# Attention scores by fp32 matmuls on 64 array rows per head in place of stacked fp32r operands

## The chip, the cores and the metric

The kernel runs on one core of one Trainium2 chip. The metric is the device time in microseconds (us), lower is better. Three runs of the kernel before gave 1060.61, 1060.61 and 1061.64 us, median 1060.61 us.

## What is computed

Three stages follow each other. The first is attention with a compressive memory, the other two are feed-forward layers on 2304 tokens of 512 channels. All data are fp32.

```python
B, H, S, D = (4, 8, 576, 64)
scores = scale * q @ k.T                      # per head, 576 x 576, causal mask
a = exp(scores - scores.max(-1)); a /= a.sum(-1) + 1e-09
local = a @ v
q_p = phi(q)                                  # elu(q) + 1
mem_out = (q_p @ M_prev) / (q_p @ z_prev + 1e-6)
x = g * mem_out + (1 - g) * local             # g = sigmoid(beta), per head
x = (h * tanh(softplus(h))) @ w_out           # h = x @ w_in, w_in 512 x 2048
out = ((x @ w1) * (x @ w2) @ w3) @ w_out2     # 512 x 1024, 1024 x 1024, 1024 x 512
```

The change concerns the line `scores` alone.

## The kernel before, in words

**The stages.** Attention works on 16 pairs of heads (`NPAIR`), one after the other in the loop `for p in range(NPAIR + 1)`. A pair holds two heads of 64 channels; transposed, head 0 lies on partitions 0 to 63 (`UP`) and head 1 on 64 to 127 (`DN`). After the loop come the feed-forward layers (`emit_h`, `emit_x2`, `fold`, `emit_ab`, `emit_out`), which the change leaves as they are.

**One turn of the loop** overlaps three pairs. For pair p it makes the scores (`s_blocks`, `s_last`) and the normalised probabilities (`normed`); for pair p-1 it transposes the probabilities (`pt_g`) and multiplies them by v (`pv`); for pair p+1 it transposes q and k (`prep_qk`) and makes phi (`prep_phi`). In turns 2 to 11 (ten turns) `steps(background, 1)` adds one block of weight decoding (`decode`, lines 92 to 105), which is work of VectorE (DVE) and GpSimd (POOL) beside attention.

**Scores of pairs 1 to 15.** `mm` (line 59) issues every matmul. An fp32r matmul makes one pass over its columns and rounds its operands, so q and k are split into a rounded part (`hq`, `hk`) and a remainder (`lq`, `lk`). Of q·k the three terms hq·hk, lq·hk and hq·lk are kept. `prep_qk` copies each transposed k from PSUM with ScalarE (ACT, line 273), and DVE forms `lk` (line 65, `sub`). For q, ACT copies it to `qt` (line 281), POOL rounds it (`hl`, line 62) and subtracts (`hl`, line 65). Then ten DMAs of 144 KB (lines 290 to 293 and 296) build operands that fill all 128 array rows: `eqk` for head 0 and `oqk` for head 1 hold [hq; lq] against [hk; hk], and `qz` holds hq with zeros in the other head's half against `lk`. So a block of 128 query rows takes two fp32r matmuls. Blocks 0 and 1 share a PSUM bank and are 256 columns wide each; blocks 2 and 3 are 384 and 512 wide. Pair 0 skips the DMAs and takes three fp32r matmuls on 64 rows per block. The last 64 queries of both heads go together (`s_last`): `qd` holds both heads' columns with zeros elsewhere, and two halves of 288 key columns take three fp32r matmuls each.

**After the matmul**, DVE adds the mask, takes the row extreme and evicts the bank (`maxed`, the CUSTOM_DVE rows of line 361); ACT applies exp and the row sum (`expd`, line 366); `normed` adds 1e-9 to the sums (DVE, line 351), takes reciprocals (line 352) and scales the probabilities (line 356, DVE or POOL). It is called three times a turn: once per head and once for the last rows.

**Queues and buffers.** Score tiles use three PSUM banks of tag A; the transposes and `pv` use the tags X (three) and F (two). The score tiles of SBUF (`s0` to `s3`) have two buffers each, and both heads of a pair share them. All DMAs are issued by SyncE (SP), in one order. The order of instructions on each engine is chosen at build time by the tile framework's scheduler; on the chip each engine follows its own list and waits on semaphores.

## Time and profile before

| | before |
|---|---|
| median of three runs | 1060.61 us |
| profiled execution (its span) | 1060.4 us |
| TensorE matmul (PE) busy | 1014.3 us, 96% |
| TensorE weight loads (PEld) busy | 877.0 us, 83% |
| VectorE (DVE) busy | 675.2 us, 64% |
| ScalarE (ACT) busy | 541.6 us, 51% |
| GpSimd (POOL) busy | 389.9 us, 37% |
| mean DMA rate | 110 GB/s |

The time is that of the one core; the profiled execution's span is 0.2 us below the median. Shares are of the whole span, and attention is only its first 277 us; the rest is feed-forward. A matmul's record runs until its last result is written, while the next may already be streaming, so the distance from start to start tells a matmul's cost in a dense stretch, and the record's length does not. An fp32 matmul leaves two records, an fp32r matmul one.

### The profile page before, as it was taken

Reading aid. Unit: us, or ns where it says so; the run is one execution under the profiler, and the core shown is the slowest. Engines: PE = TensorE matmul, PEld = TensorE weight load, DVE = VectorE, ACT = ScalarE, POOL = GpSimd, SP = SyncE. Lnnn points to the kernel's source line nnn. Section 1 sums busy time; section 2 is a strip of 40 time slices with the busy share of each in tenths; the row PEclk is TensorE's granted clock in tenths of the full one; section 3 lists DMA queues with packets and bytes.
Section 4 is the critical chain, followed back from the end, with each engine's and each line's share of the span. In section 5 each row is a group of like instructions: output and inputs, shape, how many; then the busy total and the mean of one; then the engine's idle time right before and its main releaser. Section 6 shows DMA issues by size and latency. Waiting matters only on the chain.

```text
span 1060.4 us, 17637 instructions
## 1 busy us (share of the span) xinstructions
PE 1014.3 (96%) x6360; PEld 877.0 (83%) x6360; DVE 675.2 (64%) x1630; ACT 541.6 (51%) x1128; POOL 389.9 (37%) x393
## 2 busy tenths in 40 slices
PE   6998889889999999999999999999999999999998
PEld 5665656566798999999999999999888888888897
DVE  6599999896779889888898467767632112121111
ACT  5676667677765666666666555546232122211212
POOL 7568888784345555554655211111100000000000
PEclk9999999999999999999999999999999999999999
DMA  6777777775323343334333274444150010100101
GB/s 148 170 189 184 188 187 171 167 193 123 95 64 100 120 159 101 102 123 154 113 109 106 83 257 123 145 162 130 70 179 0 1 40 1 40 1 1 40 1 60
DMA packets 115687, 116.60 MB, mean 110 GB/s; under 512 B 71952, under 2 KB 78096, under 8 KB 115600
## 3 DMA queue, kind: packets, MB, share of 16 engines
q1 hardware_dynamic: 115600, 115.48, 38.0%
q8 instruction: 50, 0.82, 0.3%
q14 instruction: 37, 0.30, 0.1%
HBM read 71.83 MB, written 21.50 MB: 88 GB/s over the span
## 4 chain that ended last, share of the span: by engine, by line
PE 60%; DVE 20%; POOL 8%; DMA 6%; issue 4%; SPq 2%; ACT 0%; POOLq 0%; DVEq 0%
PE psA L59 24%; PE psX L59 20%; PE psF L59 12%; DVE de L104 3%; POOL da L120 2%; DMA w_dram<-da 2%; DVE da L102 2%; DVE s L361 2%; POOL da L105 2%; DVE de L103 2%; PE psF L426 2%; DVE da L98 2%; DVE da L99 2%; DVE da L100 2%; DVE s L356 1%
## 5 line engine op out<-in xcount | busy, mean ns | idle before, releaser
L59 PE MATMUL psX<-gh,wqt 128*128 128x288 f32 x1024 | 209.0, 298 | 9.4 <-DVE x L579 4.7
L105 POOL TENSOR_TENSOR da<-da,de 128x512 f32<-128x512 f32 (+1 forms) x88 | 103.0, 1174 | 292.7 <-DVE de L104 270.4
L59 PEld LDWEIGHTS psX<-gh,wqt 128*128 128x128 f32 x1024 | 165.4, 189 | 13.4 <-DVE x L579 6.2
L59 PE MATMUL psX<-gl,wqt 128*128 128x288 f32 x512 | 151.2, 296 | 0.0
L59 PE MATMUL psA<-xt,wqt 128*128 128x288 f32 x840 | 122.0, 298 | 0.0
L59 PEld LDWEIGHTS psA<-xt,wqt 128*128 128x128 f32 x840 | 116.9, 191 | 3.1 <-issue 1.0
L366 ACT ACTIVATE s<-s,acc 128x512 f32<-128x512 f32 (+4 forms) x144 | 84.3, 588 | 40.4 <-DVE acc L361 34.3
L59 PEld LDWEIGHTS psX<-gl,wqt 128*128 128x128 f32 x512 | 96.9, 189 | 0.4
L98 DVE TENSOR_SCALAR da<-draw 128x512 int32<-128x512 int32 (+1 forms) x88 | 48.4, 553 | 68.7 <-POOL wqt L65 19.1
L720 ACT COPY bs<-psA 128x512 f32<-128x512 f32 (+1 forms) x40 | 21.8, 544 | 119.0 <-PE psA L59 116.6
L59 PE MATMUL psX<-wft,room 128*128 128x512 f32 x336 | 82.1, 390 | 0.0
L59 PE MATMUL psA<-x2h,w12t 128*128 128x512 f32 (+1 forms) x288 | 79.9, 354 | 0.0
L426 PE MATMUL psF<-ident,s 128*128 128x128 f32 x400 | 69.4, 288 | 9.1 <-DVE s L356 6.0
L59 PE MATMUL psF<-xt,wqt 128*128 128x288 f32 x552 | 77.3, 295 | 0.0
L487 ACT CAST gh<-y 128x576 fp32r<-128x576 f32 x64 | 43.2, 675 | 65.3 <-DVE y L484 39.7
L721 DVE TENSOR_TENSOR bs<-bs,psA 128x512 f32<-128x512 f32 (+1 forms) x20 | 12.7, 634 | 100.1 <-PE psA L59 100.1
L59 PEld LDWEIGHTS psF<-xt,wqt 128*128 128x128 f32 x552 | 74.5, 188 | 0.1
L59 PE MATMUL psX<-pt,raw 128*64 128x64 f32 (+4 forms) x576 | 74.1, 328 | 0.0
L59 PEld LDWEIGHTS psX<-wft,room 128*128 128x128 f32 x336 | 62.6, 188 | 12.6
L361 DVE CUSTOM_DVE_ANT_0 s<-psA,mask 128x512 f32<-128x512 f32 (+3 forms) x144 | 64.1, 477 | 14.0 <-PE psA L59 10.1
L428 ACT COPY pt<-psF 128x512 f32<-128x512 f32 (+1 forms) x112 | 57.2, 541 | 26.6 <-PE psF L426 25.9
L426 PEld LDWEIGHTS psF<-ident,s 128*128 128x128 f32 x400 | 48.8, 147 | 25.4 <-issue 6.2
(130 smaller groups left out, 2214.8 us busy)
## 6 DMA issues: line engine op xcount, KB each, us to landing
draw<-in_moe_w_out_dram SPq DMA_DIRECT2D x24, 512.0 KB, 3.5
draw<-in_moe_w_in_dram SPq DMA_DIRECT2D x16, 512.0 KB, 4.3
draw<-in_moe_w_dram SPq DMA_DIRECT2D x16, 512.0 KB, 4.1
draw<-in_moe_w_dram SPq DMA_DIRECT2D x32, 256.0 KB, 3.2
w12t<-w_dram SPq DMA_DIRECT2D x8, 1024.0 KB, 8.0
out_dram<-ob SPq DMA_DIRECT2D x18, 256.0 KB, 2.0
eqk<-hl SPq DMA_DIRECT2D x30, 144.0 KB, 2.6
eqk<-hk SPq DMA_DIRECT2D x30, 144.0 KB, 2.8
```

Source lines behind the costliest of these rows:

```text
L59: nc.tensor.matmul(o, lhsT=l, rhs=r, start=start, stop=stop)
L98: V.tensor_scalar(out=ai, in0=hw, scalar1=0x7FFFFFFF, scalar2=None, op0=ALU.bitwise_and)
L99: V.tensor_scalar(out=a, in0=a, scalar1=2.0 ** -15, scalar2=122879.9921875, op0=ALU.max, op1=ALU.min)
L100: V.tensor_scalar(out=ai, in0=ai, scalar1=3, scalar2=0x3FFFFFF8, op0=ALU.logical_shift_left, op1=ALU.bitwise_and)
L104: V.scalar_tensor_tensor(out=e, in0=lw.bitcast(U32), scalar=2.0 ** -52, in1=e, op0=ALU.mult, op1=ALU.mult)
L105: nc.gpsimd.tensor_tensor(out=a, in0=a, in1=e, op=ALU.add)
L361: nc.vector.tensor_tensor_reduce(out=s, in0=o, in1=m, op0=ALU.add, op1=ALU.min, scale=-scale, scalar=init, accum_out=a,)
L366: nc.scalar.activation(out=s, in_=s, func=AF.Exp, scale=-1.0, bias=a, accum_out=r)
L426: nc.tensor.transpose(o[:, 128 * x:128 * x + 128], src[:, 128 * jb:128 * jb + 128], ident)
L428: nc.scalar.copy(out=t[:, 0:n], in_=o[:, 0:n])
L487: nc.scalar.copy(out=gh, in_=y[i])
L720: nc.scalar.copy(out=bs, in_=pb)
```

## The change

Transposed q and k are kept in fp32 (`qt`, `kt`), copied from PSUM by ACT as before. Each score block of a head is one fp32 matmul on that head's 64 array rows; the two heads' matmuls are written alternately, into two banks. The rounding, the subtractions, the tiles `hl`, `hk`, `lk`, `eqk`, `oqk`, `qz` and the ten DMAs per pair are gone; pair 0 goes the same way as the others. `qd` is half as wide, and each half of `s_last` is one fp32 matmul on 128 rows. Block 0 is 128 columns wide in place of 256. The score tiles in SBUF have four buffers in place of two. `normed` is called once for all eight blocks, after the scores of both heads.

```diff
@@ -218,10 +218,6 @@
             hv = slice(64 * e, 64 * e + 64)
             nc.vector.tensor_copy(out=ogp[hv, :, 8], in_=gv[hv, :, e])
 
-    qz = ep.tile([128, 2, S], F32R, name="qz")
-    for e, hv in enumerate((DN, UP)):
-        nc.gpsimd.memset(f(qz[hv, e]), 0.0)
-
     s4 = ap_.tile([128, 640], F32, name="s4")
     nc.gpsimd.memset(s4[:, S:640], 0.0)
 
@@ -263,49 +259,16 @@
             evac(slice(c0, c1), pt[:, 0:c1 - c0])
 
     def prep_qk(p):
-        hl = ep.tile([128, 2, S], F32R, tag="hl", name="hl", bufs=1)
-        hq, lq = hl[:, 0], hl[:, 1]
-        hk = ep.tile([128, S], F32R, tag="hk", name="hk", bufs=2)
-        lk = ep.tile([128, S], F32R, tag="lk", name="lk", bufs=2)
-
-        def split(h, l):
-            def go(cs, o):
-                nc.scalar.copy(out=h[:, cs], in_=o)
-                sub(l[:, cs], o, h[:, cs])
-            return go
-
-        if p == 0:
-            trans(st[p]["q"], split(hq, lq))
-        else:
-            t = ep.tile([128, S], F32, tag="qt", name="qt", bufs=2)
-            trans(st[p]["q"], lambda cs, o: nc.scalar.copy(out=t[:, cs], in_=o))
-            pool_round(hq, t)
-            sub(lq, t, hq, nc.gpsimd)
-        trans(st[p]["k"], split(hk, lk))
-        if p > 0:
-
-            E = ep.tile([128, 2, S], F32R, tag="eo", name="eqk", bufs=2)
-            O = ep.tile([128, 2, S], F32R, tag="eo", name="oqk", bufs=2)
-            for t, a, z in ((E, UP, DN), (O, DN, UP)):
-                dm(out=f(t[a, 0]), in_=f(hq[a]))
-                dm(out=f(t[z, 0]), in_=f(lq[a]))
-                dm(out=f(t[a, 1]), in_=f(hk[a]))
-                dm(out=f(t[z, 1]), in_=f(hk[a]))
-
-            for e, hv in enumerate((UP, DN)):
-                dm(out=f(qz[hv, e]), in_=f(hq[hv]))
-            st[p]["Q"] = (E[:, 0], O[:, 0])
-            st[p]["K"] = (E[:, 1], O[:, 1])
-        st[p]["L"] = lk
-        st[p]["h"] = hl
-
-        t4 = ep.tile([128, 2, 2, 64], F32R, tag="qd", name="qd", bufs=1)
+        for nm in "qk":
+            t = ep.tile([128, S], F32, tag=nm + "t", name=nm + "t", bufs=2)
+            trans(st[p][nm], lambda cs, o: nc.scalar.copy(out=t[:, cs], in_=o))
+            st[p][nm + "t"] = t
+
+        t4 = ep.tile([128, 2, 64], F32, tag="qd", name="qd", bufs=2)
         nc.gpsimd.tensor_tensor(
-            out=t4, in0=f(hl[:, :, None, 512:S]).to_broadcast([128, 2, 2, 64]),
-            in1=own[:, None].to_broadcast([128, 2, 2, 64]), op=ALU.mult,
+            out=t4, in0=st[p]["qt"][:, None, 512:S].to_broadcast([128, 2, 64]), in1=own, op=ALU.mult
         )
-        st[p]["Q4"] = t4
-        st[p]["H"] = hk
+        st[p]["q4"] = t4
         st[p]["s"] = {}
         st[p]["sum"] = ap_.tile([128, 9], F32, tag="sum", name="sum", bufs=2)
         st[p]["acc"] = ap_.tile([128, 10], F32, tag="acc", name="acc", bufs=2)
@@ -346,7 +309,7 @@
 
         d = st[p]
         og = ogp[:, p % NP]
-        sl = slice(xs[0][1], 8, 2) if len(xs) > 1 else slice(8, 9)
+        sl = slice(0, 8) if len(xs) > 1 else slice(8, 9)
         rv = d["sum"][:, sl]
         nc.vector.tensor_scalar(out=rv, in0=rv, scalar1=1e-9, scalar2=None, op0=ALU.add)
         nc.vector.reciprocal(out=rv, in_=rv)
@@ -365,31 +328,21 @@
     def expd(s, a, r):
         nc.scalar.activation(out=s, in_=s, func=AF.Exp, scale=-1.0, bias=a, accum_out=r)
 
-    def s_blocks(p, e, blocks):
+    def s_blocks(p, blocks):
         d = st[p]
-        KL = d["L"]
-        if p > 0:
-            Q, K1 = d["Q"][e], d["K"][e]
-        r = slice(64 * e, 64 * e + 64)
-        pt = psA()
-        for j, ib in enumerate(blocks):
-            W = max(128 * ib + 128, 256)
-            o = pt[:, 256 * j:256 * j + W]
-            i_ = slice(128 * ib, 128 * ib + 128)
-            if p == 0:
-                mm(o, d["h"][r, 0, i_], d["H"][r, 0:W], True, False)
-                mm(o, d["h"][r, 1, i_], d["H"][r, 0:W], False, False)
-                mm(o, d["h"][r, 0, i_], KL[r, 0:W], False, True)
-            else:
-                mm(o, Q[:, i_], K1[:, 0:W], True, False)
-                mm(o, qz[:, e, i_], KL[:, 0:W], False, True)
+        pt = [psA() for _ in range(2)]
         for j, ib in enumerate(blocks):
             W = 128 * ib + 128
-            s = ap_.tile([128, W], F32, tag=f"s{ib}", name=f"s{ib}", bufs=2)
-            x = 2 * ib + e
-            maxed(s, pt[:, 256 * j:256 * j + W], mask[:, 384 - 128 * ib:512], 3e38, d["acc"][:, x:x + 1])
-            expd(s, d["acc"][:, x:x + 1], d["sum"][:, x:x + 1])
-            d["s"][ib, e] = s
+            for e, r in enumerate((UP, DN)):
+                mm(pt[e][:, 256 * j:256 * j + W], d["qt"][r, 128 * ib:128 * ib + 128], d["kt"][r, 0:W], True, True)
+        for j, ib in enumerate(blocks):
+            W = 128 * ib + 128
+            for e in range(2):
+                s = ap_.tile([128, W], F32, tag=f"s{ib}", name=f"s{ib}", bufs=4)
+                x = 2 * ib + e
+                maxed(s, pt[e][:, 256 * j:256 * j + W], mask[:, 384 - 128 * ib:512], 3e38, d["acc"][:, x:x + 1])
+                expd(s, d["acc"][:, x:x + 1], d["sum"][:, x:x + 1])
+                d["s"][ib, e] = s
 
     def s_last(p):
         d = st[p]
@@ -398,9 +351,7 @@
         for z in range(2):
             o = psA()[:, 0:CH]
             cs = slice(CH * z, CH * z + CH)
-            mm(o, d["Q4"][:, 0].rearrange("p e c -> p (e c)"), d["H"][:, cs], True, False)
-            mm(o, d["Q4"][:, 1].rearrange("p e c -> p (e c)"), d["H"][:, cs], False, False)
-            mm(o, d["Q4"][:, 0].rearrange("p e c -> p (e c)"), d["L"][:, cs], False, True)
+            mm(o, d["q4"].rearrange("p e c -> p (e c)"), d["kt"][:, cs], True, True)
             maxed(s[:, cs], o, mask4 if z else mask[:, 0:CH], acc[:, 9:10] if z else 3e38, acc[:, 9 - z:10 - z])
         expd(s, acc[:, 8:9], d["sum"][:, 8:9])
         d["s"][4] = s4
@@ -508,21 +459,17 @@
             ek.close()
             wps[0] = wk.enter_context(tc.tile_pool(name="wp", bufs=1, side="right"))
         if now:
-            s_blocks(p, 0, (3,))
+            s_blocks(p, (3,))
         if old:
             for i in (4, 2, 3):
                 pt_g(p - 1, i)
         if new:
             prep_qk(p + 1)
         if now:
-            s_blocks(p, 0, (2,))
+            s_blocks(p, (2,))
             if p == 0:
                 prep_phi(0)
-            s_blocks(p, 0, (0, 1))
-            normed(p, [(i, 0) for i in range(4)])
-            s_blocks(p, 1, (0, 1))
-            s_blocks(p, 1, (3,))
-            s_blocks(p, 1, (2,))
+            s_blocks(p, (0, 1))
         if p + 2 < NPAIR:
             load_pair(p + 2)
         if old:
@@ -532,11 +479,11 @@
                 emit_h((0, 0, 0))
             pt_g(p - 1, 6)
         if now:
+            normed(p, [(i, e) for e in range(2) for i in range(4)])
             pt_g(p, 1)
         if 2 <= p < 12:
             steps(background, 1)
         if now:
-            normed(p, [(i, 1) for i in range(4)])
             s_last(p)
         if old:
             pv(p - 1)
```

The first place is TensorE in a turn of the steady stretch, before the change: the scores of head 1 (`oqk`, `lk`/`qz`), the last rows (`qd`), and the next pair's head 0 (`eqk`); `psF<-ident,s` are transposes of probabilities, `psX<-pt,raw` are `pv`.

```order
L59 MATMUL psA<-lk,qz 128x256
L59 MATMUL psA<-oqk 128x256
L59 MATMUL psA<-lk,qz 128x256
L59 MATMUL psX<-pt,raw 64x64 x7
L59 MATMUL psA<-oqk 128x512
L59 MATMUL psA<-lk,qz 128x512
L59 MATMUL psX<-pt,raw 64x64
L262 MATMUL psX<-ident,raw 128x128 x2
L59 MATMUL psA<-oqk 128x384
L59 MATMUL psA<-lk,qz 128x384
L59 MATMUL psX<-pt,raw 64x64 x2
L59 MATMUL psA<-hk,qd 128x288 x2
```

And TensorE in a turn of the changed kernel, with buffer numbers: `psA_1152` and `psA_1153` are the 512-wide blocks of the two heads of one pair, `psA_1207` and `psA_1208` the 384-wide ones.

```order
L59 MATMUL psA_1152<-kt_988,qt_978 128x512
L377 MATMUL psF_1053<-ident_66,s4_114 128x128
L59 MATMUL psX_1093<-pt_971,raw_433 64x384
...
L258 MATMUL psX_1144<-ident_66,phie_1126 128x128 x3
L59 MATMUL psA_1153<-kt_988,qt_978 128x512
L59 MATMUL psA_1207<-kt_988,qt_978 128x384
L59 MATMUL psA_1208<-kt_988,qt_978 128x384
L258 MATMUL psX_1184<-ident_66,raw_1030 128x128 x2
```

The number of score matmuls per pair (without the last rows) falls from 16 to 8. The two heads of a block do not always stand side by side: the 512-wide blocks here have 27 other matmuls between them, since the second waits for a bank, while head 1's 512 columns and head 0's 384 do follow each other. Over the whole attention the 128 score matmuls of 64 rows stand in 59 runs.

The second place is SP's queue in turn 2 to 3, before:

```order
L296 DMA qz<-hl 64x576 x2
L244 DMA raw<-in_q_dram 128x4x64 x2
L246 DMA raw<-in_q_dram 128x2x64
L244 DMA raw<-in_k_dram 128x4x64 x2
L290 DMA eqk<-hl 64x576
L291 DMA eqk<-hl 64x576
```

And the same queue now:

```order
L92 DMA draw<-in_moe_w_in_dram 128x1024
L240 DMA raw<-in_v_dram 128x4x64 x2
L246 DMA raw<-in_v_dram 64x2x64 x2
L240 DMA raw<-in_q_dram 128x4x64 x2
L242 DMA raw<-in_q_dram 128x2x64
L249 DMA zr<-in_z_prev_dram 128x128
```

The loads of q, k, v, z and of the weights (`draw`) no longer stand behind copies that wait for POOL and TensorE.

## Rows read from the trace of the kernel before

**Rows 1.** Busy time by stretch: us, busy of each engine, PEclk, DMA share, GB/s.

```profile
0.00:50.00 50.00, 40.05 (x211) 29.91 (x211) 30.98 (x98) 31.06 (x82) 33.73 (x50) 0.97 0.69 161
50.00:225.00 175.00, 154.00 (x1006) 104.05 (x1005) 162.78 (x451) 117.22 (x338) 138.26 (x143) 0.97 0.76 183
225.00:277.00 52.00, 50.06 (x352) 35.91 (x351) 38.72 (x135) 38.95 (x115) 26.14 (x30) 1.00 0.49 117
277.00:1060.00 783.00, 770.17 (x4797) 707.16 (x4795) 442.74 (x950) 354.32 (x594) 191.79 (x172) 1.00 0.27 90
```

**Rows 2.** Timeline of DVE, the eviction that ends the scores of pairs 2, 11, 15.

```profile
61.42 0.51 DVE L361 CUSTOM_DVE_ANT_0 s<-psA,mask,acc 128x288 f32<-128x288 f32 x1
...
219.38 0.51 DVE L361 CUSTOM_DVE_ANT_0 s<-psA,mask,acc 128x288 f32<-128x288 f32 x1
...
277.00 0.51 DVE L361 CUSTOM_DVE_ANT_0 s<-psA,mask,acc 128x288 f32<-128x288 f32 x1
```

**Rows 3.** Groups by line on DVE, 20 to 275 us: busy, mean ns, idle before.

```profile
L65 DVE TENSOR_TENSOR lk<-psX,hk 128x256 fp32r<-128x256 f32 (+1 forms) x30 | 12.9, 441 | 4.8 <-ACT hk L273 4.7
```

**Rows 4.** Groups by line and shape on DVE, 50 to 225 us.

```profile
L351 DVE TENSOR_SCALAR sum<-sum 128x4 f32<-128x4 f32 x20 | 10.7, 537 | 1.2 <-ACT s L366 1.2
...
L352 DVE RECIPROCAL sum<-sum 128x4 f32<-128x4 f32 x20 | 3.4, 170 | 0.2
```

**Rows 5.** Line 351 alone: duration min/median/max in ns.

```profile
L351 DVE TENSOR_SCALAR sum<-sum x48: 118/160/1390, 17.6 to 279.1; 128x4 f32<-128x4 f32 x32, 128x1 f32<-128x1 f32 x16
```

**Rows 6.** Groups by line on POOL, 20 to 275 us.

```profile
L65 POOL TENSOR_TENSOR hl<-qt,hl 128x576 fp32r<-128x576 f32 x15 | 22.0, 1464 | 0.7
...
L303 POOL TENSOR_TENSOR qd<-hl,own 128x256 fp32r<-128x256 f32 x15 | 13.1, 874 | 1.9 <-PE psF L426 1.3 <-DMA oqk<-hl 0.5
...
L62 POOL TENSOR_SCALAR hl<-qt 128x576 fp32r<-128x576 f32 x15 | 10.7, 716 | 7.0 <-ACT qt L281 4.4 <-DMA oqk<-hl 1.2 <-issue 1.2
```

**Rows 7.** Timeline of PE, a dense run of scores: start, length, record.

```profile
271.98 0.28 PE L59 MATMUL psA<-lk,qz 128*128 128x256 f32 x1
272.10 0.40 PE L59 MATMUL psA<-oqk 128*128 128x512 f32 x1
272.33 0.40 PE L59 MATMUL psA<-lk,qz 128*128 128x512 f32 x1
272.56 0.34 PE L59 MATMUL psA<-oqk 128*128 128x384 f32 x1
272.74 0.34 PE L59 MATMUL psA<-lk,qz 128*128 128x384 f32 x1
...
275.26 0.29 PE L59 MATMUL psA<-lk,qd 128*128 128x288 f32 x1
275.39 0.43 PE L59 MATMUL psA<-hk,qd 128*128 128x288 f32 x2
```

**Rows 8.** Timeline of PE, fp32 matmuls of `pv` and transposes.

```profile
152.10 1.13 PE L59 MATMUL psX<-phi,mr 128*128 128x512 f32 x2
153.15 1.07 PE L59 MATMUL psX<-pt,raw 128*64 128x512 f32 x2
...
154.86 1.07 PE L59 MATMUL psX<-pt,raw 128*64 128x512 f32 x4
...
157.37 0.28 PE L426 MATMUL psF<-ident,s 128*128 128x128 f32 x1
157.58 0.54 PE L59 MATMUL psX<-pt,raw 128*64 128x384 f32 x2
```

**Rows 9.** DMA issues: count, KB each, median us to landing.

```profile
eqk<-hl SPq DMA_DIRECT2D x30, 144.0 KB, 2.6
```

**Rows 10.** Waits of SP's queue, whole span: us in total, times, longest.

```profile
SPq L290 <- PE psA L59: 22.7, 20, 3.8
```

**Rows 11.** Waits of all engines, 20 to 275 us.

```profile
PE psA L59 <- DMA eqk<-hk: 2.4, 3, 1.0
```

**Rows 12.** The chain that ended last, its longest DMA piece in attention.

```profile
141.59 5.88 DMA eqk<-hk
```

## The prediction

> **What bounds the kernel now.** I read the busy times by stretch first. They split the span in four [rows 1]: a start of 50 us, a steady stretch of attention from 50 to 225 us, the end of attention to 277 us, and the feed-forward layers. In the last, TensorE is busy 770.17 of 783 us; the change touches nothing there, so I take it as a block of fixed length, and attention's gain or loss passes on in full. Inside attention the bound changes. From 50 to 225 us DVE is busiest, 162.78 of 175 us (93%), TensorE has 154.00 (88%), POOL 138.26. From 225 to 277 us TensorE has 50.06 of 52 us and DVE 38.72: no weight decoding is left in those turns.
>
> The timeline gives a turn's length [rows 2]. The last eviction of pair 2's scores stands at 61.42 us, that of pair 11 at 219.38: nine turns of 17.55 us, with decoding. From there to pair 15 at 277.00 are four turns of 14.4 us, without. So of a turn of 17.55 us DVE is busy 0.93 x 17.55 = 16.3. TensorE's busy share overstates it, since a record is about 0.28 us long where the next one starts 0.12 us later [rows 7]; what a turn costs TensorE when little holds it up is 50.06/52 x 14.4 = 13.9 us. DVE with 16.3 is the bound of ten turns, TensorE with 13.9 that of the last four, and about 1.2 us of each decoding turn is stall.
>
> **What leaves DVE.** Per pair the two subtractions for `lk` go: 30 took 12.9 us [rows 3], so 0.86 us. One of the two `normed` calls for the blocks goes, with a 128x4 addition and a reciprocal: 537 and 170 ns in the steady stretch [rows 4], so 0.71 us. The addition alone shows how much of this is waiting: its median is 160 ns and its longest 1390 ns [rows 5], and it reads and writes SBUF only, beside a POOL that is busy 79% of the stretch [rows 1]. POOL loses the rounding, the subtraction and half of `qd`: 22.0 + 10.7 + 13.1/2 = 39 us over 15 pairs [rows 6], 2.6 us of the 13.9 us that it is busy per turn. How much DVE gains from a quieter POOL no row tells. It may be nothing, and at most all 2.6 us. I take 0.5: the addition lost 537 - 160 = 377 ns twice per turn, other DVE operations on SBUF must lose too, and a fifth of POOL's work goes. DVE then has 16.3 - 0.86 - 0.71 - 0.5 = 14.2 us per decoding turn.
>
> **What TensorE does in place of it.** Before: from start to start an fp32r matmul of 512 columns takes 0.23 us, of 384 0.18, of 256 0.12, of 288 0.13 [rows 7]. A head is 2 x 0.23 + 2 x 0.18 + 4 x 0.12 = 1.30 us, the last rows 6 x 0.13 = 0.78, a pair 3.4 us. For sixteen pairs that is 54 us (pair 0, with three terms, costs more, but stands in the start, where TensorE has time).
>
> After: an fp32 matmul of 512 columns leaves two records, which keep TensorE from 152.10 to 153.15 and from 153.15 to beyond 154.16, so 1.0 us [rows 8]. A part of this is a change of tile shape: transposes on 128x128 follow each other every 0.11 us, but from the one at 157.37 to the first 128x64 matmul at 157.58 there are 0.21 us [rows 8], so a change of shape costs 0.10. Without it 512 columns take 0.87 us or 1.7 ns per column. Counted in the order, the 128 score matmuls have 40,960 columns: one after the other 70 us. The last rows add 32 x 288 columns, 15.7 us. Changes of shape between neighbours rise from 158 to 262 in attention, 104 x 0.10 = 10.4 us. Sum: 96 us.
>
> Against this stands that two heads use different halves of the array's rows. Whether such matmuls run at the same time no row shows. The nearest is `pv`, where the heads use different halves of the columns: two matmuls, 512 and 384 wide, end 1.07 us after the first starts, as long as one of 512 alone needs (two and four records, both 1.07 us) [rows 8]. So I take full overlap inside a run. In the order, where runs are broken by waits for banks, overlap leaves about 30,000 of the 40,960 columns: 51 us. Then TensorE has 51 + 15.7 + 10.4 = 77 us in place of 54, 23 us more, 1.4 us per pair; without overlap 96 - 54 = 42 us, 2.6 per pair. The Trainium skill, "TensorEngine Tiling (Array Packing)", section "Theoretical Speedup", gives up to 2x for a contraction of 64 or less; by that the 70 us would be 35, and the sum below would come out some 7 us faster. The order speaks against this: only heads that stand next to each other can share the array.
>
> **What leaves the queues.** 150 DMAs of 144 KB go [rows 9], each half a microsecond of SP's time. SP's queue stood 22.7 us in 20 waits on TensorE before `eqk` could be overwritten [rows 10], and the loads of raw q and k and of weights stood behind. TensorE itself waited for these copies only 2.4 us in three places [rows 11], yet one of them is 5.88 us of the chain that ended last [rows 12]. The chain shows no sum that I may subtract: where a copy is gone, an eviction or exp is late next. I count this as part of the stall, with the two further score buffers, which let a pair's evictions start before the transposes of the previous pair have read theirs. ACT has the same copies as before, so nothing there.
>
> **The sum.** In the ten decoding turns DVE falls to 14.2 us, and TensorE rises to 13.9 + 1.4 = 15.3 us and becomes the longer one. With the old stall of 1.2 us a turn takes 16.5. But now two engines are nearly equally full, and scores, evictions, exp and transposes hand work to and fro between them; a stall of 1.5 is as likely, for the copies' latency is gone at the same time. I take 16.8: 0.75 us less per turn, -7.5 us. The last four turns were TensorE's: 4 x 1.4 = +5.6 us, of which about 1 us returns from the copies. The start (pairs 0 and 1) has 10 us in which TensorE stands still [rows 1], some of it while the first copies are built; I take -3 us there, with the price of 2 x 1.4 us inside what is idle. Together -7.5 + 4.6 - 3 = -6 us against the profiled span of 1060.4. It lies 0.2 us below the median of the runs, so 1060.6 - 6 = **1054.6 us**. Between a stall of 0.7 and one of 2 us per turn the forecast's own range is 1047 to 1059.
>
> **The rivals.** A difference of 0.2% is 2.1 us, about what a measurement of this kernel can tell from no change.
>
> *TensorE takes the place of DVE* (slower). The place is the score runs; the price is that the two heads don't overlap, or that the second mostly waits for its bank until the first is done. Then a turn has 13.9 + 2.6 = 16.5 us of TensorE; with 1.2 us of stall it is 17.7, as now, the last four turns cost 4 x 2.6 = 10 us and the start 2: 1073 us. With overlap and a stall of 2.5 us per decoding turn the ten turns gain nothing, and 1063 comes out. It decides from the point where TensorE's addition exceeds some 2 us per decoding turn. For it: the fp32 passes are plain in the rows, and TensorE is at 96% in the last turns. Against it: the `pv` rows.
>
> *The full gain.* The queues and POOL were the real cause of the stall, and the array overlaps more than the order suggests, or hides its changes of shape. Then a decoding turn falls to about 15.5 us, -20 us, the last turns stay as they are, and the start gives 3: 1037 us. For it: the 5.88 us of one copy on the chain, and DVE additions of up to 1390 ns. Against it: 104 more changes of shape. A doubling as the page on tiling has it would lie between this case and mine.
>
> *Nothing to measure.* Gains in ten turns and losses in the others cancel, or POOL and DVE give their time to ACT's exp: 1060.6 within 2 us.
>
> **How the numbers follow.** My forecast 45%, the full gain 13%, nothing 12%, slower 30%. Of the forecast's range almost all lies more than 2.1 us below the median. So faster 0.57, same 0.12, slower 0.31. For eight in ten the range must reach into both other cases: down to 1038, where the full gain ends, and up to 1074, past the case without overlap.
>
> **What the changed profile would show.** Right: attention ends 5 to 10 us sooner; from 50 to 225 us DVE falls below 88% busy and TensorE rises above it; line 351's mean shrinks; the two heads' matmuls start within a few tens of ns of each other where they are neighbours, and both end together; a DMA share of about 0.4 in place of 0.76. Wrong: the second head's records start only when the first head's end; turns of 17 us and more with TensorE near 96%; or turns below 15.5 us; or a feed-forward part whose length changes by more than 2 us.

## The result, and the profile after

The changed kernel takes 1049.32 us (median of four runs, 1048.44 to 1049.86) against 1061.05 us of the kernel before on the same chip (1060.61 to 1061.64). The ratio is 0.9893, with an interval from 0.9879 to 0.9907: 11.7 us less. The sign and the range of the prediction hold; the gain is about twice the 6 us that it named. The profiled execution has a span of 1048.1 us, before 1060.4; the last window below ends behind the changed program's end.

Busy time by stretch of the changed kernel, columns as in [rows 1]:

```profile
0.00:50.00 50.00, 42.67 (x194) 24.68 (x194) 36.18 (x102) 30.06 (x84) 34.48 (x49) 1.00 0.57 135
50.00:225.00 175.00, 175.00 (x1097) 104.39 (x1096) 151.40 (x441) 129.78 (x378) 110.39 (x127) 1.00 0.39 96
225.00:277.00 52.00, 51.62 (x339) 33.14 (x338) 29.55 (x97) 34.23 (x93) 14.19 (x19) 1.00 0.13 38
277.00:1060.00 783.00, 754.83 (x4693) 694.94 (x4693) 436.17 (x926) 344.70 (x577) 186.38 (x168) 1.00 0.27 88
```

From 50 to 225 us TensorE goes from 154.00 of 175 us busy to all 175.00, DVE from 162.78 to 151.40 (87%), POOL from 138.26 to 110.39, and the DMA share from 0.76 to 0.39. The granted clock goes from 0.97 to 1.00. The chain of waits inside attention says the same without the weakness of busy shares. First the kernel before, then the change, both cut to 20 to 265 us, shares by line (PE is TensorE; `psA` are scores, `psX` with L59 `pv` and the memory's matmuls, `psF` and the other `psX` transposes):

```profile
by line: PE psA L59 11.6%; PE psX L59 9.7%; DVE s L361 8.4%; DVE s L356 6.4%; PE psF L426 5.9%; issue 5.4%; PE psX L262 4.0%; DMA draw<-in_moe_w_in_dram 3.4%; DVE phie L323 2.9%; DVE da L102 2.7%; DVE dn L329 2.4%; DVE sum L351 2.4%; DMA eq
```

```profile
by line: PE psX L59 34.6%; PE psA L59 32.7%; PE psF L377 20.7%; PE psX L258 12.1%; issue 0.0%
```

Before, no engine carries the chain: TensorE's four groups here are 31%, and DVE, DMAs and issue alternate with them. After, the four groups of TensorE are the whole of it. One engine, never waiting, now sets the length of attention.

The evictions that end the scores of pairs 2, 11 and 15, in DVE's timeline of the change [rows 2]:

```profile
58.71 0.51 DVE L324 CUSTOM_DVE_ANT_0 s<-psA,mask,acc 128x288 f32<-128x288 f32 x1
...
200.84 0.52 DVE L324 CUSTOM_DVE_ANT_0 s<-psA,mask,acc 128x288 f32<-128x288 f32 x1
...
263.80 0.52 DVE L324 CUSTOM_DVE_ANT_0 s<-psA,mask,acc 128x288 f32<-128x288 f32 x1 [2.66 <-PE psF L377]
```

Pair 2 ends 2.7 us sooner. The nine decoding turns up to pair 11 take (200.84 - 58.71)/9 = 15.79 us each in place of 17.55, together 15.8 us less. The last four take 62.96/4 = 15.74 us in place of 14.4, together 5.3 us more. Turns with and without decoding are equally long now: decoding is hidden. Attention ends 13.2 us sooner, more than the 5 to 10 us that the prediction named as its sign; what follows takes 784.3 in place of 783.4 us.

TensorE's timeline of the change shows the overlap (start, length, operation, and how many records stand in the row; one head's fp32 matmul leaves two):

```profile
150.71 1.12 PE L59 MATMUL psA<-kt,qt 64*128 64x512 f32 x2
...
154.52 0.33 PE L59 MATMUL psX<-pt,raw 128*64 128x64 f32 x2
154.78 0.33 PE L377 MATMUL psF<-ident,s 128*128 128x128 f32 x1
155.03 0.33 PE L59 MATMUL psX<-pt,raw 128*64 128x64 f32 x2
...
167.30 1.13 PE L59 MATMUL psA<-kt,qt 64*128 64x512 f32 x4
```

Two records of one head take 1.12 us, four records of both heads 1.13 us: two heads on opposite halves of the rows cost as much as one. The three rows between show the price of changing shape: matmuls of 64 columns and transposes alternate every 0.26 us, while transposes in a row follow each other every 0.11 us [rows 8]. So a change costs some 0.15 us here, not the 0.10 us of the prediction.

That holds for the whole timeline. Divide TensorE's records between the evictions of pairs 2 and 15 into runs of one tile shape. A run lasts longer than its columns take in a dense stretch, by a median of 0.16 us for 128x128 tiles, 0.15 for 128x64 and 0.20 for 64x128 (runs without overlap), or about 0.16 per change. The prediction had only the wait before the next matmul's start; the first matmul after a change is longer as well.

### The profile page after: what moved, and what is told of

Its sections match the earlier page's. It is cut to its first block, busy times and chain, and to the rows that moved or that the text cites. A ratio compares the mean times of both kernels' runs of the same rounds, so it can differ in the third digit from the quotient of the medians.

```text
span 1048.1 us, 17122 instructions
## 1 busy us (share of the span) xinstructions
PE 1024.1 (98%) x6320; PEld 857.2 (82%) x6320; DVE 653.3 (62%) x1564; ACT 538.8 (51%) x1128; POOL 345.4 (33%) x361
## 4 chain that ended last, share of the span: by engine, by line
PE 75%; DVE 12%; POOL 6%; issue 3%; DMA 2%; ACT 1%; SPq 1%; DVEq 0%; POOLq 0%
PE psA L59 29%; PE psX L59 25%; PE psF L59 12%; PE psF L377 5%; PE psX L258 3%; POOL da L120 2%; DVE de L104 2%; POOL da L105 2%; DVE da L99 1%; DVE da L100 1%; DVE de L103 1%; DVE gl L65 1%; DVE da L98 1%; DVE da L102 1%; DMA w_dram<-da 1%
## 5 line engine op out<-in xcount | busy, mean ns | idle before, releaser
L59 PE MATMUL psX<-gh,wqt 128*128 128x288 f32 x1024 | 208.4, 297 | 11.9 <-DVE x L524 6.2
L59 PEld LDWEIGHTS psX<-gh,wqt 128*128 128x128 f32 x1024 | 164.7, 188 | 16.1 <-DVE x L524 7.4
L59 PE MATMUL psX<-gl,wqt 128*128 128x288 f32 x512 | 150.7, 295 | 0.0
L59 PE MATMUL psA<-xt,wqt 128*128 128x288 f32 x840 | 121.8, 297 | 0.6 <-DVE y L435 0.6
L59 PEld LDWEIGHTS psA<-xt,wqt 128*128 128x128 f32 x840 | 116.3, 190 | 3.7 <-DVE y L435 1.5
L329 ACT ACTIVATE s<-s,acc 128x384 f32<-128x384 f32 (+3 forms) x144 | 84.8, 593 | 36.4 <-DVE acc L324 22.1
L59 PEld LDWEIGHTS psX<-gl,wqt 128*128 128x128 f32 x512 | 96.5, 188 | 0.4
L59 PE MATMUL psX<-wft,room 128*128 128x512 f32 x336 | 82.1, 390 | 0.0
L59 PE MATMUL psA<-x2h,w12t 128*128 128x512 f32 (+1 forms) x288 | 79.9, 354 | 0.0
L324 DVE CUSTOM_DVE_ANT_0 s<-psA,mask 128x512 f32<-128x512 f32 (+2 forms) x144 | 65.0, 478 | 21.3 <-PE psA L59 19.1
L59 PE MATMUL psF<-xt,wqt 128*128 128x288 f32 x552 | 77.3, 295 | 0.0
L59 PE MATMUL psX<-pt,raw 128*64 128x64 f32 (+4 forms) x576 | 75.0, 328 | 0.0
L59 PE MATMUL psA<-kt,qt 64*128 64x384 f32 (+3 forms) x256 | 71.6, 490 | 3.0 <-DVE acc L324 2.5
L59 PEld LDWEIGHTS psF<-xt,wqt 128*128 128x128 f32 x552 | 74.5, 188 | 0.1
L59 PEld LDWEIGHTS psX<-wft,room 128*128 128x128 f32 x336 | 62.6, 188 | 12.6
L59 PE MATMUL psA<-x2s,w12t 128*128 128x512 f32 x288 | 67.9, 389 | 0.0
```

The lines of the kernel that those rows point to most:

```text
L59: nc.tensor.matmul(o, lhsT=l, rhs=r, start=start, stop=stop)
L324: nc.vector.tensor_tensor_reduce(out=s, in0=o, in1=m, op0=ALU.add, op1=ALU.min, scale=-scale, scalar=init, accum_out=a,)
L329: nc.scalar.activation(out=s, in_=s, func=AF.Exp, scale=-1.0, bias=a, accum_out=r)
```

## The experiments

The theory after the result was that TensorE alone sets a turn, so that its own list decides: score columns left after overlap, at 1.7 ns each, and changes of tile shape between neighbours, at 0.10 us each (both prices from the prediction, and so in the expectations). The rivals were that one of the other parts carries the gain: the score buffers, the copies, POOL's work, DVE's work. Each variant's list was counted over attention. "Pair 2" is when its scores end, the turns are worked out as above, and "half clock" is the work that TensorE lost there to its lower clock, the sum over the turns between the evictions of pairs 0 and 15 of their length times (1 - granted clock). The last column is the counted list against the changed kernel's, with a change at 0.10 us and, behind the stroke, at the measured 0.16. The kernel before, measured beside each variant, took between 1058.96 and 1061.46 us, and the ratio is to that; so differences of two variants' medians, unless they were measured side by side, are good to some 2.5 us.

| kernel | median us | ratio to before [interval] | pair 2 | decoding turn | last turns | changes / columns | half clock | counted, 0.10 / 0.16 |
|---|---|---|---|---|---|---|---|---|
| before | 1061.05 | | 61.42 | 17.55 | 14.41 | 158 / | 6.8 | |
| changed | 1049.32 | 0.9893 [0.9879, 0.9907] | 58.71 | 15.79 | 15.74 | 262 / 30,336 | 0 | 0 |
| two buffers | 1069.96 | 1.0095 [1.0068, 1.0121] | 60.16 | 17.29 | 16.82 | 285 / 34,304 | 0 | +9 / +10 |
| old order, 2 buffers | 1065.19 | 1.0062 [1.0042, 1.0082] | 56.98 | 17.44 | 17.12 | 271 / 40,704 | 0 | +18.5 / +19 |
| old order, 4 buffers | 1051.20 | 0.9925 [0.9896, 0.9954] | 58.37 | 15.82 | 16.24 | 219 / 37,376 | 0 | +7.6 / +5 |
| 128 rows | 1050.63 | 0.9907 [0.9887, 0.9927] | 57.96 | 16.23 | 15.66 | 144 / 40,960 | 0 | +6 / -1 |
| copies back | 1057.07 | 0.9962 [0.9948, 0.9975] | 62.55 | 16.40 | 15.45 | 242 / 32,000 | 0 | +1 / 0 |
| POOL back | 1058.57 | 0.9992 [0.9970, 1.0015] | 64.68 | 16.91 | 15.53 | 247 / 30,720 | 6.8 | -1 / -2 |
| DVE back | 1051.55 | 0.9919 [0.9884, 0.9954] | 59.58 | 15.99 | 15.95 | 269 / 29,056 | 3.4 | -1.5 / -1 |
| decoding to 15 | 1048.82 | 0.9900 [0.9874, 0.9926] | 58.40 | 15.96 | 15.55 | 261 / 30,976 | 0 | +1 / +1 |
| before, less room | 1072.83 | 1.0117 [1.0084, 1.0149] | 62.85 | 18.29 | 14.93 | 140 / | 13.7 | |
| the same, 4 buffers | 1072.37 | 1.0106 [1.0073, 1.0138] | 65.64 | 17.92 | 15.63 | 150 / | 10.2 | |
| before, 3 buffers | 1074.95 | 1.0144 [1.0116, 1.0172] | 60.90 | 18.85 | 15.23 | 140 / | 13.7 | |
| two `s4` | 1046.69 | 0.9869 [0.9853, 0.9886] | 53.25 | 16.08 | 15.39 | 217 / 27,008 | 1.7 | -10 / -13 |

### Two score buffers again

```diff
-                s = ap_.tile([128, W], F32, tag=f"s{ib}", name=f"s{ib}", bufs=4)
+                s = ap_.tile([128, W], F32, tag=f"s{ib}", name=f"s{ib}", bufs=2)
```

> The changed kernel with two buffers for each score tile again, nothing else. Theory (TensorE bounds every turn of the changed kernel): what counts is the order that the buffers allow. It has 285 changes of tile shape in place of 262 and some 34,300 columns with overlap in place of 30,300, so TensorE gets 2.3 + 6.8 = 9 us more work and the time is about 1058 us. Rival (the gain came from DMAs and DVE, the buffers did nothing): 1049 us, within 2.

It takes 1069.96 us: 20.6 us more than the change, slower than the kernel before, and 12 us above the expected 1058. The waits of all engines, first the changed kernel from 20 to 265 us, then this one from 20 to 275 (total, times, longest):

```profile
DVE s L324 <- PE psA L59: 18.2, 19, 2.1
...
DVE s L324 <- PE psF L377: 4.6, 3, 2.7
```

```profile
DVE s L324 <- PE psF L377: 39.1, 20, 2.7
...
DVE s L324 <- PE psA L59: 25.2, 15, 2.3
```

The eviction waits 39.1 us in place of 4.6 for `psF`, that is for the transposes (line 377) that read the old contents of its score tile. The counted list explains 9 or 10 of the 20.6 us. TensorE's timeline says where the rest is: from pair 2's to pair 15's eviction this kernel takes 17.8 us more than the changed one. The runs of score matmuls last 60.6 us in place of 48.2, so 12.4 us are overlap lost and changes of shape; 3.4 us are TensorE standing still. TensorE's four groups are 82% of this kernel's chain in attention, so evictions that come late have a part in it.

### The operands alone, in the order of before

Scores are made head by head and `normed` is called once per head, as before, but by fp32 matmuls on 64 rows; then the same with four buffers.

```diff
-    def s_blocks(p, blocks):
+    def s_blocks(p, e, blocks):
...
-            s_blocks(p, (0, 1))
+            s_blocks(p, 0, (0, 1))
+            normed(p, [(i, 0) for i in range(4)])
+            s_blocks(p, 1, (0, 1))
+            s_blocks(p, 1, (3,))
+            s_blocks(p, 1, (2,))
```

> The fp32 operands alone: the changed kernel's qt and kt, no copies, but the scores written head by head, two buffers per score tile and normed per head, as before. In this order no two heads' matmuls overlap (40,700 of 40,960 columns one after the other). Theory (the operands free DVE, POOL and the queues, but only with four buffers per score tile can TensorE be kept busy; the x1 run lost 20 us with two): no better than the kernel before, 1058 to 1070 us. Rival (removing copies, POOL's and DVE's work is the whole gain, whatever the buffers): 1052 us or less.

> As y1_old_order, with four buffers per score tile: fp32 operands, head by head. 219 changes of tile shape in place of 262, and 37,400 columns in place of 30,300 after overlap. Theory (buffers decide, overlap and changes of shape about cancel, as in x4_128rows): 1049 to 1054 us. Rival (the overlap of the two heads carries the gain): TensorE has 12 - 4 = 8 us more, 1057 us and up.

With two buffers 1065.19 us: without the buffers and without the alternation, the new operands lose 0.6%, although the copies and the work of POOL and DVE are gone. With four buffers, measured beside it, it takes 1051.20 us, 14.0 less; both as expected. The chain of the first, 20 to 265 us, is TensorE alone, as in the changed kernel:

```profile
by line: PE psA L59 37.4%; PE psX L59 31.4%; PE psF L376 19.8%; PE psX L258 11.5%
```

So here the buffers don't act by ending a wait on the chip. With more buffers the build time's scheduler writes another order for TensorE: 52 fewer changes of shape and 3,328 fewer columns outside an overlap, counted 5.2 + 5.7 = 10.9 of the 14.0 us, and 8.3 + 5.7 = 14.0 at the measured 0.16 us per change.

### The scores without overlap

`qt` holds each head's q with zeros in the other half, written by two ACT copies of 64 partitions. Each head is one fp32 matmul on all 128 rows.

```diff
-                mm(pt[e][:, 256 * j:256 * j + W], d["qt"][r, 128 * ib:128 * ib + 128], d["kt"][r, 0:W], True, True)
+                mm(pt[e][:, 256 * j:256 * j + W], d["qt"][:, e, 128 * ib:128 * ib + 128], d["kt"][:, 0:W], True, True)
```

> The changed kernel with q kept with zeros in the other head's half, so that each score matmul is fp32 on all 128 rows: no overlap of heads, but no change of tile shape for scores either. Theory (overlap is worth 70 - 51 = 19 us of TensorE, the 118 changes of shape that go are worth 12): 7 us slower, about 1056 us, with TensorE without idle time. Rival 1 (TensorE is not the bound): 1049 within 2. Rival 2 (changes of shape cost more than their 0.10 us, by draining the queue): faster than 1049.

It takes 1050.63 us, 1.3 more than the change, with intervals that overlap; I had expected 7 more. All 40,960 columns are paid for (18 us more), but the score matmuls now have the shape of the transposes and 118 changes go: 11.8 us less at 0.10 us each, which leaves 6 us that are not there, but 18.9 at the measured 0.16. So the second rival was right that a change costs more than 0.10 us, though the kernel is not faster. The first rival's time came out too, but not its reason: TensorE is busy 144.91 of the 146.0 us of the decoding turns. Here 512 columns take 0.86 us from start to start, 152.16 to 153.02, without a change on either side; in the changed kernel it was 1.06, 150.71 to 151.77, with one on each:

```profile
152.16 1.02 PE L59 MATMUL psA<-kt,qq 128*128 128x512 f32 x2
153.02 0.27 PE L390 MATMUL psF<-ident,s 128*128 128x128 f32 x1
```

The overlap is real, but what it saves here is paid back in shape changes.

### The copies back

Ten DMAs of 144 KB per pair into tiles that nobody reads.

```diff
+            for g in range(2):
+                w = ep.tile([128, 2, S], F32, tag="cp", name="cp", bufs=2)
+                for nm, j in (("qt", 0), ("kt", 1)):
+                    dm(out=w[UP, j], in_=st[p][nm][UP])
+                    dm(out=w[DN, j], in_=st[p][nm][DN])
+            for hv in (UP, DN):
+                dm(out=cq[hv], in_=st[p]["qt"][hv])
```

> The changed kernel with ten copies of 144 KB per pair from qt and kt into tiles that nothing reads: the old load on SP's queue and on the DMA engines, without anyone who waits for the copies. Theory (the copies cost only through those who waited for them): within 2 us of 1049. Rival (the load itself and the loads queued behind it made the stall of 1.2 us per turn): turns of 17 us again, 10 us or more slower, 1059 us and up.

It takes 1057.07 us, 7.8 more, between the two expectations, with a counted list hardly longer. Nobody reads the copies, so their cost comes through the queue and its order: SP waits 11.5 us in nine places for ACT's copy of k before it may issue a copy, and the loads stand behind. Line 98, the first DVE operation of decoding, by shape from 50 to 225 us (busy, mean ns, idle before), in the changed kernel and here:

```profile
L98 DVE TENSOR_SCALAR da<-draw 128x512 int32<-128x512 int32 x8 | 4.0, 502 | 0.1
```

```profile
L98 DVE TENSOR_SCALAR da<-draw 128x512 int32<-128x512 int32 x10 | 5.2, 517 | 9.9 <-DMA draw<-in_moe_w_in_dram 6.3 <-DMA draw<-in_moe_w_dram 2.5 <-DMA draw<-in_moe_w_out_dram 0.7
```

DVE now stands 9.9 us for raw weights that queue behind the copies. The three longest pieces of the chain, 20 to 265 us, are a copy and two such loads:

```profile
51.21 8.03 DMA cp<-qt
...
143.34 4.80 DMA draw<-in_moe_w_out_dram
...
178.84 6.05 DMA draw<-in_moe_w_dram
```

### POOL's work back

POOL rounds q and subtracts, as before, into a tile that nobody reads.

```diff
+        if p > 0:
+            w = ep.tile([128, 2, S], F32R, tag="pw", name="pw", bufs=1)
+            pool_round(w[:, 0], st[p]["qt"])
+            sub(w[:, 1], st[p]["qt"], w[:, 0], nc.gpsimd)
```

> The changed kernel with POOL's rounding and subtraction of q back (2.1 us per pair), results unread. Theory (TensorE is the bound, DVE has about 2 us of slack per turn): at most 3 us slower, 1049 to 1052. Rival (a busy POOL stretches DVE's work on SBUF and DVE is still close to the bound): DVE's 128x8 addition and the scalings get longer, turns grow by 0.5 to 1 us, 1057 to 1063 us.

It takes 1058.57 us, 9.3 more, as the rival had it, with a list counted 1 or 2 us shorter. The profiled execution is 7 us above this median: its clock was 0.50 from 45 to 59 us, which the other turns don't show, so only turns after pair 2 are compared. They give 9 x 1.12 - 4 x 0.21 = 9.2 us, about the whole difference. The nine decoding turns, first of the changed kernel, then here, columns as above:

```profile
58.70:200.80 142.10, 142.10 (x899) 85.44 (x899) 127.61 (x366) 105.73 (x306) 95.70 (x110) 1.00 0.41 102
```

```profile
64.70:216.90 152.20, 145.61 (x913) 86.89 (x909) 141.01 (x368) 105.22 (x306) 113.49 (x123) 1.00 0.38 96
```

TensorE stands still for 6.6 us, and DVE is busy 13.4 us more with as many operations of its own program, at 93% of the time, the share that it had in the kernel before. Two DVE operations of decoding, by shape from 50 to 225 us, in the changed kernel and here:

```profile
L102 DVE SCALAR_TENSOR_TENSOR da<-draw,da 128x512 int32<-128x512 int32 x9 | 10.2, 1128 | 0.1
...
L104 DVE SCALAR_TENSOR_TENSOR de<-draw,de 128x512 f32<-128x512 uint32 x9 | 6.0, 664 | 0.0
```

```profile
L102 DVE SCALAR_TENSOR_TENSOR da<-draw,da 128x512 int32<-128x512 int32 x9 | 12.4, 1373 | 0.1
...
L104 DVE SCALAR_TENSOR_TENSOR de<-draw,de 128x512 f32<-128x512 uint32 x9 | 9.2, 1023 | 0.0
```

Both take longer, by 245 and 359 ns, though DVE's own program has not changed. Not all do: the 128x8 addition, which the rival named, takes 247 ns in place of 266, and the scaling of 384 columns 689 in place of 811. Over all, DVE's operations are slower beside a busier POOL; but DVE's order was chosen anew too, and the runs don't separate the price of this from work queued behind POOL's two steps.

### DVE's subtractions back

```diff
+                if nm == "k":
+                    nc.vector.tensor_tensor(out=w[:, cs], in0=o, in1=t[:, cs], op=ALU.subtract)
```

> The changed kernel with DVE's two subtractions of k per pair back, results unread (0.86 us of DVE per pair). Theory (DVE and TensorE are now nearly equally full, so every DVE microsecond counts in part, as POOL's 2.1 us counted 9 us in x3_pool): 4 to 9 us slower, 1053 to 1058 us. Rival (TensorE alone bounds the turns): 1049 within 2.

It takes 1051.55 us, 2.2 more; the ratio's interval overlaps the changed kernel's, so the effect is small or nothing. I had expected 4 to 9: DVE has 15.79 - 14.2 = 1.6 us of room per turn now, and 0.86 us fit into it.

### Decoding spread to the last turns

```diff
-        if 2 <= p < 12:
+        if 2 <= p < 16:
```

> The changed kernel with one block of weight decoding in turns 12 to 15 too. Theory (in those turns TensorE is the bound and DVE has over 6 us free per turn, so the decoding costs nothing there; the feed-forward part then has four blocks less to decode while TensorE waits some 16 us in it): 2 to 6 us faster, 1043 to 1047 us. Rival (the decoding costs as much in attention as in the earlier turns, and the feed-forward part gains nothing): 1049 to 1054 us.

It takes 1048.82 us, 0.5 less, which is no difference. Turns with and without decoding were already equal, so attention stays as long (264.22 against 263.80), and what follows shortens by 2.3 us in this profile, 782.0 against 784.3. The 2 to 6 us that I had expected did not come.

### Four buffers with the stacked operands

With the stacked operands kept, four buffers don't fit: the pool of attention's early tiles then wants 55.3 KB per partition where 46.3 are left. To have room I took a buffer each from `qt`, `phie`, raw q/k and raw v of the kernel before (less room), and added the score buffers to that. A third kernel takes `qt` and `phie` alone and has three score buffers.

```diff
-                a = ap_.tile([128, NB, 2, D], F32, tag="vr", name="raw", bufs=3)
+                a = ap_.tile([128, NB, 2, D], F32, tag="vr", name="raw", bufs=2)
...
-            t = ep.tile([128, S], F32, tag="qt", name="qt", bufs=2)
+            t = ep.tile([128, S], F32, tag="qt", name="qt", bufs=1)
```

> The kernel before with 9.75 KB per partition freed: one buffer in place of two for qt and for phi's exp, three in place of four for raw q and k, two in place of three for raw v. Only the control for z1_room_4. Both theories: 1059 to 1065 us, no faster than before.

> z0_room with four buffers per score tile: stacked fp32r operands and copies as before, the buffers of the changed kernel. Theory (the kernel before is bound by DVE, 93% busy, which waits for a score buffer only 2.9 us in all; the buffers help only where TensorE is the bound, as between y1 and y3): within 3 us of z0_room. Rival (the buffers are the whole gain, whatever the operands, and the stacked ones even cost TensorE less): 10 us or more faster than z0_room, 1051 us or less.

> The kernel before with three buffers per score tile, room made by one buffer in place of two for qt and for phi's exp alone. Theory: within 3 us of the kernel before. Rival: 5 us or more faster than before.

Room alone costs 11 us against the kernel before beside it (1061.46), where I had expected at most 4, so the comparison stands on a disturbed base. On it, four buffers give nothing: 1072.37 against 1072.83 us, as the theory had it. The kernel with three takes 1074.95, 13.5 more than the kernel before, and not within 3. The stretch from 50 to 225 us, first with less room alone, then with four buffers, columns as above:

```profile
50.00:225.00 175.00, 154.22 (x993) 105.34 (x994) 153.63 (x437) 115.22 (x330) 127.10 (x134) 0.94 0.73 173
```

```profile
50.00:225.00 175.00, 152.63 (x998) 102.93 (x998) 151.81 (x435) 113.73 (x326) 128.40 (x135) 0.96 0.70 170
```

TensorE and DVE stay at 87 to 88% busy and the clock falls below 1.00. Here something other than score buffers holds the turns: fewer buffers for raw data, the copies and POOL's work are all there, and which of them it is is not shown. Whether the kernel before would gain from four buffers with nothing taken from it stays open, since there is no room for it.

### A second buffer for the last rows

`s4`, the score tile of the last 64 queries, was the one left with a single buffer.

```diff
-    s4 = ap_.tile([128, 640], F32, name="s4")
+    s4_ = [ap_.tile([128, 640], F32, name=f"s4{i}") for i in range(2)]
...
-        s = s4[:, 0:S]
+        s = s4_[p % 2][:, 0:S]
```

> The changed kernel with two buffers in place of one for the probabilities of the last 64 queries (s4). Theory (TensorE is the bound in all turns of the changed kernel, and a further score buffer acts through the order that it allows): 217 changes of tile shape in place of 262 and 27,000 columns in place of 30,300, so TensorE has 4.5 + 5.6 = 10 us less; DVE, at 87%, then takes a part of it back, 1039 to 1045 us. Rival (TensorE is not what bounds the turns, or the order's counts say little of the time): 1049 within 2.

It takes 1046.69 us, 0.9869 of before, the best of all; but the interval overlaps that of the change, and I had expected 1039 to 1045. Pair 2 ends 5.5 us sooner. Attention ends at 259.55 us in place of 263.80, and what follows takes 786.8 us in place of 784.3. Two of the nine decoding turns take 17.5 and 19.6 us; the busy times of about these two stretches:

```profile
84.00:102.00 18.00, 16.28 (x96) 10.23 (x95) 17.24 (x42) 11.07 (x35) 12.02 (x15) 0.91 0.44 107
102.00:122.00 20.00, 18.82 (x114) 10.58 (x115) 18.21 (x49) 13.14 (x38) 12.80 (x15) 1.00 0.39 95
```

In the first DVE is busy 17.24 us and TensorE 16.28, with 3.4 us at half clock. Shorten TensorE's list by a counted 10 us, and TensorE waits again in some turns, with DVE the busier engine in one of them; that DVE binds them is likely, but not shown.

## Why the prediction came out as it did

**The bound.** Right: TensorE takes over all turns. Its last four turns went from 14.4 to 15.74 us, +1.34 where the sum of 51 + 15.7 + 10.4 us had said +1.4 per pair. This agreement is in part luck. The last four turns, before and after:

```profile
219.40:277.00 57.60, 54.50 (x372) 38.30 (x371) 44.32 (x151) 42.73 (x127) 30.36 (x36) 1.00 0.52 122
```

```profile
200.80:263.80 63.00, 63.00 (x404) 38.54 (x404) 35.76 (x131) 44.26 (x130) 20.74 (x27) 1.00 0.12 27
```

TensorE's busy time rose by 2.1 us per turn, and 0.8 us of idle time went. The assumed overlap, for which there were only the `pv` rows, holds for neighbours. The start with pair 2 gave 2.7 us; the forecast was 3 and, for pair 2's turn, 0.75. The feed-forward part changed by 0.9 us, within the 2 allowed.

**The terms that were mis-sized** are the stall of the decoding turns and the change of shape, in opposite directions. TensorE was put at 15.3 us and a stall of 1.5 on top, for 16.8; measured are 15.79. The stall is gone: TensorE is busy in all 142.10 us of these nine turns. TensorE's own turn is longer than 15.3, for a change of shape costs 0.16 us and not 0.10: the 104 more of them are 16.6 us in place of 10.4, the sum per pair is 1.8 in place of 1.4, and 13.9 + 1.8 = 15.7. The prediction's own rows held a sign of it: the 512 columns from 152.10 to 153.15 take 1.05 us with a change behind them [rows 8], 0.18 more than the 0.87 without. Nine turns gave 15.8 us in place of 6.8, and this error of 9 us is more than the 6 us by which the profiled span differs from the forecast; the start, the last turns and the feed-forward part gave some back, 1.0, 0.7 and 0.9 us.

**The step behind it.** The prediction said that now "two engines are nearly equally full" and hand work to and fro, and so kept a stall of 1.5 us; but DVE, busy 90% of these turns, never made TensorE wait. The kernel with two buffers has such long turns, 17.29 us with decoding, but not for that reason alone: its last turns, where DVE is busy 56% of the time, take 16.82. The step that failed is the one that counted the two further score buffers only "as part of the stall", with no price. They are worth 14 us with the old order and 20.6 with the new one, more than the whole gain, and in both cases much of it is the order of TensorE's list and not a wait that ends. They come with the operands: the removed tiles leave the SBUF that they need. Without them the new operands are slower than the old ones.

**DVE** fell to 87% as forecast (below 88%), and its 127.61 us in nine turns are the forecast's 14.2 us per turn, but by a wrong reason in part. The one `normed` for eight blocks does add and invert cheaply, by shape from 50 to 225 us of the change:

```profile
L319 DVE TENSOR_SCALAR s<-s,sum,ogp 128x384 f32<-128x384 f32 x22 | 17.8, 811 | 0.0
...
L314 DVE TENSOR_SCALAR sum<-sum 128x8 f32<-128x8 f32 x11 | 2.9, 266 | 1.2 <-ACT s L329 1.2
...
L315 DVE RECIPROCAL sum<-sum 128x8 f32<-128x8 f32 x11 | 2.2, 200 | 0.1
```

The addition takes 266 ns in place of 537 [rows 4], once in place of twice. But stretched operations are not gone: line 319 still needs 811 ns for 384 columns, and line 102 1128 ns.

**The rest of the list.** The removed loads were priced as small terms of DVE's turn or of a stall, yet two of them are worth several microseconds when put back alone: copies 7.8, POOL 9.3. DVE's subtractions are worth about 2, which the runs don't tell from nothing. They don't add up to the gain, and needn't: TensorE is the bound only as long as every other part stays below it. So the theory that its list alone decides is too simple. With a change at 0.16 us it comes within some 3 us for the old order with two and four buffers, the 128 rows and the decoding to 15; it does not explain the copies, POOL, half of the effect of two buffers, or how little the second `s4` gave.

**The rivals.** That the heads would not overlap is ruled out by the rows at 150.71 and 167.30. The full gain (turns of 15.5 us, 1037 us) came near in the decoding turns, 15.79, but it had the last turns stay as they were. The Trainium skill, "TensorEngine Tiling (Array Packing)", section "Theoretical Speedup", has up to 2x; for neighbours the rows agree (1.13 and 1.12 us), while over the list 30,336 of 40,960 columns are left. By that page the prediction put its sum some 7 us faster; worked out with its own terms, as an estimate, the step from 51 to 35 us is 1.0 us per pair, so up to 14 us in the fourteen turns that TensorE bounds. The run lies 5 us below the forecast, but the doubling is not the reason, since the scores without overlap cost only 1.3 us.

**Open**: how much of POOL's 9.3 us is slower DVE operations; whether the buffers alone would help the stacked operands; and what the clock gives (below). The scheduler writes a new order for every variant, so no run changes one thing alone.

## What to carry to other kernels

Ask of every removed tile what buffers the freed SBUF allows, and price those as a part of their own: here they decide between a loss and a gain. Where a scheduler orders the work, count from its order the changes of tile shape and the neighbours that can overlap; price a change from a whole run of one shape and not from one gap. More matmul work on one engine can still win if that engine never waits. When two engines are near each other, put back each removed load by itself before calling it hidden.

## What the runs showed of the hardware

**A stall of TensorE can cost twice.** I had counted the kernel before's idle time as idle time alone. Its busy time by microsecond, columns as above:

```profile
112.00:113.00 1.00, 0.75 (x8) 0.36 (x6) 1.00 (x2) 1.00 (x4) 1.00 (x2) 1.00 0.97 184
113.00:114.00 1.00, 0.00 (x0) 0.00 (x0) 1.00 (x2) 0.26 (x2) 1.00 (x2) 1.00 1.00 244
114.00:115.00 1.00, 0.84 (x3) 0.46 (x4) 1.00 (x5) 0.00 (x0) 1.00 (x2) 0.97 1.00 205
115.00:116.00 1.00, 1.00 (x4) 0.58 (x4) 1.00 (x2) 0.00 (x0) 1.00 (x2) 0.50 0.73 147
116.00:117.00 1.00, 0.73 (x5) 0.71 (x5) 1.00 (x5) 0.36 (x1) 0.83 (x2) 0.50 0.24 58
117.00:118.00 1.00, 1.00 (x6) 1.00 (x6) 1.00 (x5) 1.00 (x4) 0.08 (x1) 0.50 0.20 58
118.00:119.00 1.00, 1.00 (x4) 0.40 (x3) 1.00 (x5) 0.80 (x2) 1.00 (x2) 0.82 0.83 201
```

TensorE stands still from 113 to 114 us, and a microsecond later its granted clock is 0.50, the lower of its two levels (1.2 in place of 2.4 GHz), for about 3.4 us. That happens three times in the nine decoding turns and once in the start. Not every stall is followed by it: in the same trace TensorE stands still for 1.15 us from 123.3 us on, and with the copies back for 1.96 us from 57.5 us on, and the granted clock stays 1.00. Length times (1 - granted clock) over the nine turns is 5.1 us; in the changed kernel, whose TensorE is busy throughout that stretch, it is 0. So at most 5.1 of the 15.8 us are clock, and the rest is not; no run here fixes the clock alone, and it is not shown how much of it lay on the path.

**Row halves share the array fully** in fp32 for neighbours: 1.13 us for both heads, 1.12 for one; the second head's records start 7 ns after the first's. **A change of tile shape** costs 0.15 to 0.20 us in these kernels, and at 0.16 the 262 of them are some 42 us of attention.
